# Loading q and v for two pairs of heads at once, copying the unit matrix on chip, halving the last output block, and writing the whole order out

## The chip, the cores and the metric

The kernel runs on one core of a Trainium2 chip. Five engines work side by side, each through its own list of instructions in a fixed order: TensorE (PE; PEld are its weight loads), VectorE (DVE), ScalarE (ACT), GpSimd (POOL) and SyncE (SP), which here does nothing but issue DMAs. The metric is the device time of one execution in microseconds. Three runs of the kernel before took 343.11, 344.51 and 344.69 us, median 344.51.

## The reference

The inputs are q, k and v of 4 batches with 8 heads of 576 rows and 64 columns, a routing matrix `moe_phi`, two expert weights and two weights of a dense layer. Three steps follow each other:

```
attn = softmax(mask(q @ k.T / 8)) @ v        # window of 32; heads 4 to 7: every 4th position of 128
x    = attn laid out as (2304, 512)
logits = x @ phi                             # 32 slots, 8 experts of 4
slots  = softmax(logits, over tokens).T @ x
out_s  = relu(slots @ w1[e]) @ w2[e]         # w1: 8 x 512 x 1024, w2: 8 x 1024 x 512
x    = softmax(logits, over slots) @ out_s   # (2304, 512)
h    = x @ w_in                              # w_in (512, 2048), w_out (2048, 512) in 64 bits
out  = silu(h) @ w_out
```

## The kernel before

**Stages.** The first stage is attention over 16 pairs of heads, n = 0 to 15. For each pair three loads bring k, q and v, 288 KB each (`lk`, `lq`, `lv`: lines 167, 171, 184); POOL and DVE spread q over two halves (`qx`, `qy`, line 180) and v (`vx`, `vy`, lines 197 to 201); PE adds a mask and multiplies (`M`, `S`); DVE takes the row maximum (`rm`, line 227); ACT exponentiates nine blocks (`ex`, line 232); DVE inverts the sums (`rc`, lines 244 and 245), POOL scales (`nm`, line 249), DVE transposes in four pieces (`pt`, lines 256 to 263); PE multiplies by v (`pv`); ACT copies out (`xe`), PE transposes with a unit matrix (`T`, line 312), ACT copies again (`te`). In between the logits of a batch are reduced over tokens (`da` to `ds`) and over slots: `cad` (lines 412 to 414) takes the sum over slots and its inverse, `caf` and `cag` make two parts, `cb` transposes them on PE (line 434) and `cbs` copies them into the tile `ct`. The second stage is the experts: `L1.0` to `L1.15` and `L2.0` to `L2.15` on PE, each with one 1024 KB weight tile (`lw1`, `lw2`, lines 530 and 536; the last tile of w2 in three parts, `lw2.15`, `lw2b`, `lw2c`). The third is the dense layer. Its 64-bit weights come in by `lwi` and `lwo` (lines 620, 625), DVE turns them into 32-bit numbers in three passes (lines 634, 636, 638: `cva`, `cvb`, `cvi` for w_in and `cvc`, `cvd`, `cvo` for w_out), PE multiplies w_in by the expert outputs (`aqh0`, `aq0`, `aqr0`, later `aq1`, `aq3`, ...; rows `w_wif,lg`), ACT and DVE write the result in two parts (`ah`, `al`), and PE forms h in blocks (`h`, `ch`; rows `ct_ct,rv_astk`) and the products with w_out (`on`, `om`, and `pp` for the last 1536 tokens, where sums of weights and activations replace eight products by seven).

**What sets the order.** Each engine runs its instructions in the order in which they are emitted. Up to the middle of the experts that order comes from a list scheduler in the kernel file (costs, a table of bonuses); from `L2.5` on it is written out as a list of names, `LATER`. The loads stand in a list of their own. A load waits for its place in SBUF: the slots of raw q, k and v are reused after two to five pairs, those of the weights after the tile that was there before.

**Unit matrix and end.** One load, `cip` (line 1174), brings a 128x256 tile `ip`: phi, and a 128x128 unit matrix in 32 bits. The same matrix in 16 bits comes with the mask (`cmask`, line 1123). At the end two 128x384 blocks are summed by DVE (`pe1.6.0`, `pe1.6.1`, line 1116) and each is stored by one DMA (line 1119).

Of the kernel before, what the change touches and what calls it, by code (L numbers as in the profile page):

```python
# [32 lines left out]
def fused_kernel(ctx: ExitStack, tc: tile.TileContext, a: dict):  # L33
# [298 lines left out]
    for n in range(NPAIR):  # L332
        b, p = divmod(n, 4)
        kb, rb = before(kslot, n), before(rslot, n)
        qb, vb = before(qslot, n), rb if n < NPAIR - 1 else None
# [1 line left out]
        op(f"lq{n}", "SP", .74, [f"qx{qb}", f"qy{qb}"] if qb is not None else [], lambda n=n: load_q(n))
        op(f"lv{n}", "SP", .74, [f"vx{vb}", f"vy{vb}"] if vb is not None else [], lambda n=n: load_v(n))
        for z in range(2):
            op(f"q{'xy'[z]}{n}", "DVE" if z and n not in QP else "POOL", .7, [f"lq{n}", f"S{n-2}" if n >= 2 else None], lambda n=n, z=z: spread(n, z))  # L340
        for z in range(2):
            op(f"v{'xy'[z]}{n}", veng(n) if z else "POOL", {"POOL": 1.4, "ACT": .68, "DVE": .745}[veng(n) if z else "POOL"], [f"lv{n}", f"pv{n-2}.1" if n >= 2 else "izm", ("nm0", "rc0")[z] if n == 1 else None], lambda n=n, z=z: vmask(n, z))
# [838 lines left out]
    op("crs", "POOL", .9, ["cip", "nm3"], crs)  # L1181


    wl_ = [f"lw1.{i}" for i in range(16)] + [f"lw2.{i}" for i in range(16)] + ["lw2b", "lw2c"]
    il = [f"lwi0.{k}" for k in range(2)]
    ol = ["lwo0", "lwo1"]
    loads = ["lq0", "lk0", "cmask", "lq1", "lk1", "cip", "lv0", "lq2", "lk2", "lv1"]
    vs = [f"lv{n}" for n in range(2, NPAIR)]
    n = 3
    for c in ATT:  # L1190
        if c == "q":
            loads += [f"lq{n}", f"lk{n}"]
            n += 1
        else:
            loads.append({"w": wl_, "v": vs, "i": il, "o": ol}[c].pop(0))
    assert n == NPAIR and not vs + wl_ + il + ol
    loads += ["lwi1.0", "lwo2", "lwi2.0", "lwo4", "lwi3.0", "lwo6", "lwi4.0", "lwo8", "lwi5.0", "lwo10", "lwi6.0", "lwo12", "lwi7.0", "lwo14"]
    assert len(loads) == len(set(loads)) == sum(o[0] == "SP" for n, o in ops.items()) - 6 - 16
    for x, y in zip(loads, loads[1:]):
        ops[y][2].append(x)  # L1200
# [69 lines left out]
LATER = """  # L1270
L2.5 cb2.1 cbs2.1 L2.6 ht1 lwo1 cb2.0 hr1 L2.7 lwi0.0 cvc0 L2.8 L2.9 cvd0 caf3 lw2.14 cvc1 L2.10 cva0.0 lw2.15 lw2b L2.11 ani L2.12 cvo0
cbs2.0 wh0 cvb0.0 L2.13 cvd1 wl0 L2.14 lw2c cvo1 L2a lwi0.1 cvi0.0 lwi1.0 L2b wh1 lwo2 wl1 L2.15 cag3 ts0.1 soe0 cb3.1 soe1 ts0.2 lwi2.0
ts0.4 th0.2 cva0.1 sotm0 sote0 sotm1 aqh0 tl0.2 sote1 cvb0.1 aq0 cvi0.1 ah0 al0 aqr0 h0.0.0 gh0.0.0 h0.0.1 cva1.0 ahr0 gh0.0.1 si0.0.0
cvb1.0 alr0 si0.0.1 cvi1.0 cvc2 on0.0.0 gl0.0.0 on0.2.0 lwo4 cb3.0 on0.1.0 h0.1.0 aq1 gh0.0.2 cbs3.1 lwi3.0 cbs3.0 si0.0.2 gl0.0.1 h0.1.1
om0.0.0 ah1 cvd2 gl0.0.2 ac2.0 gh0.1.0 cvo2 om0.1.0 on0.5.0 om0.2.0 on0.3.0 om0.3.0 si0.1.0 gl0.1.0 ac2.1 wh2 cva2.0 on0.4.0 om0.4.0 lwo6
am1 om0.5.0 al1 om0.0.1 ac2.2 ac3.0 ac2.3 ac3.3 wl2 om0.1.1 om0.2.1 h0.2.0 cva3.0 ac3.1 h0.2.1 om0.3.1 om0.4.1 gh0.2.0 om0.5.1 cvb2.0
on0.1.2 cvb3.0 si0.2.0 gl0.2.0 on0.0.2 ac3.2 on0.3.2 h0.3.0 h0.3.1 om0.0.2 on0.5.2 on0.2.2 si0.3.0 om0.1.2 gh0.3.0 om0.2.2 cvi3.0 cvi2.0
cvc4 om0.3.2 gl0.3.0 aq3 ah3 on0.4.2 om0.4.2 am3 om0.5.2 om0.0.3 om0.1.3 ac4.1 cvd4 al3 cvo4 lwi4.0 cva4.0 lwo8 cvc6 ac4.2 om0.2.3 ac5.1
ac4.0 ac5.3 ac4.3 wh4 h0.4.0 h0.4.1 gh0.4.0 ac5.0 om0.3.3 ac5.2 om0.4.3 wl4 om0.5.3 si0.4.0 cvd6 on0.5.4 on0.1.4 ac7.0 ac6.2 h0.5.0 gl0.4.0
h0.5.1 lwi5.0 gh0.5.0 cvo6 on0.0.4 si0.5.0 gl0.5.0 ac6.3 ac6.0 wh6 on0.3.4 om0.0.4 on0.4.4 om0.1.4 on0.2.4 om0.2.4 om0.3.4 cvb4.0 ac6.1  # L1280
om0.4.4 om0.5.4 wl6 ac7.3 om0.0.5 h0.6.0 h0.6.1 gh0.6.0 si0.6.0 cvi4.0 om0.1.5 om0.2.5 ac7.2 gl0.6.0 cva5.0 om0.3.5 om0.4.5 cvb5.0 lwo10
ac7.1 om0.5.5 h0.7.0 h0.7.1 om0.0.6 om0.1.6 om0.2.6 gh0.7.0 si0.7.0 om0.3.6 cvi5.0 aq5 cvc8 gl0.7.0 cvd8 ah5 cvc10 om0.4.6 cvo8 am5 al5
lwi6.0 ac8.0 ac8.2 ac8.3 ac9.0 om0.5.6 ac8.1 om0.0.7 om0.1.7 wh8 ac9.1 lwo12 om0.2.7 h0.8.0 h0.8.1 om0.3.7 si0.8.0 om0.4.7 om0.5.7 gh0.8.0
ts2.1 cvd10 ac10.3 ac9.3 ac9.2 wl8 cvo10 on0.2.8 on0.0.8 gl0.8.0 ac11.3 ac10.2 h0.9.0 h0.9.1 on0.1.8 gh0.9.0 ts1.1 on0.5.8 on0.4.8 om0.0.8
# [237 lines left out]
```

## Time and profile before

| what | us |
|---|---|
| three runs | 343.11, 344.51, 344.69 |
| the profiled execution, its own time | 343.64 |
| its span in the trace | 341.5 |
| PE busy in the span | 329.4 (96%) |
| DVE busy | 263.3 (77%) |
| ACT busy | 221.9 (65%) |
| POOL busy | 74.6 (22%) |

Around the span lie 2.1 us (343.64 less 341.5). The profiled execution is 0.9 us under the median of the three runs, and between the fastest and the slowest of them. Ends of matmuls are modelled in the trace, so a busy PE can hide a short wait; the start times of the next rows tell it.

### The profile page before, as it was taken

Reading aid. Unit: us, or ns where it says so; the run is one execution under the profiler, and the core shown is the slowest. Engines: PE = TensorE matmul, PEld = TensorE weight load, DVE = VectorE, ACT = ScalarE, POOL = GpSimd, SP = SyncE. Lnnn points to the kernel's source line nnn. Section 1 sums busy time; section 2 is a strip of 40 time slices with the busy share of each in tenths; the row PEclk is TensorE's granted clock in tenths of the full one; section 3 lists DMA queues with packets and bytes.
Section 4 is the critical chain, followed back from the end, with each engine's and each line's share of the span. In section 5 each row is a group of like instructions: output and inputs, shape, how many; then the busy total and the mean of one; then the engine's idle time right before and its main releaser. Section 6 shows DMA issues by size and latency. Waiting matters only on the chain.

```text
span 341.5 us, 8179 instructions
## 1 busy us (share of the span) xinstructions
PE 329.4 (96%) x3221; PEld 272.1 (80%) x3232; DVE 263.3 (77%) x479; ACT 221.9 (65%) x639; POOL 74.6 (22%) x121
## 2 busy tenths in 40 slices
PE   7998999999899999999999999999999999999995
PEld 3687877777633337788888888999999999999995
DVE  5777877689660099999999997989994654999573
ACT  3599989797430125778496999996467666645540
POOL 6987978675260000000000000000000000000000
PEclk9999999999999999999999999999999999999999
DMA  7999999999999999818390000110200011000004
GB/s 259 405 405 406 403 401 407 416 404 415 416 405 423 416 411 419 349 58 322 125 356 15 0 0 2 55 68 2 77 3 0 0 71 69 3 23 23 2 22 147
DMA packets 17893, 70.03 MB, mean 205 GB/s; under 512 B 1984, under 2 KB 4288, under 8 KB 12096
## 3 DMA queue, kind: packets, MB, share of 16 engines
q1 hardware_dynamic: 17856, 69.53, 51.9%
q8 instruction: 25, 0.41, 0.5%
q14 instruction: 12, 0.10, 0.1%
HBM read 64.80 MB, written 4.72 MB: 204 GB/s over the span
## 4 chain that ended last, share of the span: by engine, by line
PE 83%; DMA 8%; DVE 3%; ACT 2%; POOL 1%; issue 1%; DVEq 0%; ACTq 0%; POOLq 0%
PE ps L86 80%; DMA w_w2.13_1760<-in_w 5%; PE ps L312 3%; DMA w_wi<-in_w_in 3%; ACT rt_px L232 1%; DMA rs_raw<-in_q 1%; POOL rv_v L1138 1%; ACT rt_px L301 1%; POOL rb_a L180 0%; PE ps L434 0%; POOL ra_a L180 0%; ACT x_xb L315 0%; DVE stats L227 0%; DVE csm L413 0%; DVE spaced L244 0%
## 5 line engine op out<-in xcount | busy, mean ns | idle before, releaser
L1083 DVE TENSOR_TENSOR rt_stl<-w_raww,rs_sth 128x768 fp32r<-128x768 f32 (+1 forms) x52 | 42.2, 830 | 18.2 <-ACT rs_sth L1081 17.9
L86 PE MATMUL ps<-w_ws,x_gz 128*128 128x512 f32 x216 | 53.6, 393 | 0.0
L86 PE MATMUL ps<-rs_sth,w_ws 128*128 128x384 f32 x192 | 53.1, 334 | 0.0
L1081 ACT CAST rs_sth<-w_raww 128x768 fp32r<-128x768 f32 (+1 forms) x52 | 37.8, 738 | 22.3 <-PE ps L86 16.6
L232 ACT ACTIVATE rt_px<-ps,spaced 128x64 f32<-128x64 f32 x144 | 43.5, 332 | 10.2 <-DVE spaced L228 8.5
L86 PEld LDWEIGHTS ps<-w_ws,x_gz 128*128 128x128 f32 x216 | 40.0, 188 | 7.7 <-issue 0.4
L86 PEld LDWEIGHTS ps<-rs_sth,w_ws 128*128 128x128 f32 x192 | 35.1, 188 | 0.0
L232 ACT ACTIVATION_READ_ACCUMULATOR rt_px<-ps,spaced 128x1 f32 x144 | 32.3, 225 | 0.0
L86 PE MATMUL ps<-rt_stl,w_ws 128*128 128x384 f32 x96 | 32.1, 334 | 0.0
L86 PE MATMUL ps<-ct_ct,rv_astk 128*128 128x384 f32 x96 | 27.3, 338 | 0.0
L1066 ACT ACTIVATE w_raww<-ps 128x384 f32<-128x384 f32 x48 | 22.0, 493 | 7.1 <-PE ps L86 7.0
L249 POOL TENSOR_TENSOR rt_px<-rt_px,stats 128x576 f32<-128x576 f32 (+2 forms) x17 | 18.6, 1093 | 8.2 <-DVE stats L245 3.4
L86 PEld LDWEIGHTS ps<-ct_ct,rv_astk 128*128 128x128 f32 x96 | 17.6, 188 | 2.4 <-issue 0.4
L86 PEld LDWEIGHTS ps<-rt_stl,w_ws 128*128 128x128 f32 x96 | 18.0, 188 | 0.0
L896 ACT ACTIVATE x_gz<-ps 128x768 fp32r<-128x768 f32 (+3 forms) x18 | 13.3, 740 | 4.8 <-PE ps L86 4.7
L899 DVE TENSOR_TENSOR x_gz<-rt_gtm,x_gz 128x768 fp32r<-128x768 f32 (+3 forms) x18 | 15.5, 864 | 1.0 <-ACT rt_gtm L889 0.9
L1081 ACT CAST rs_sth<-x_rawx 128x768 fp32r<-128x768 f32 x12 | 10.0, 837 | 9.6 <-PE ps L86 6.3
L889 ACT ACTIVATE rt_gtm<-ps 128x768 f32<-128x768 f32 (+3 forms) x18 | 13.2, 742 | 3.8 <-PE ps L86 3.6
L86 PEld LDWEIGHTS ps<-ra_a,rv_v 128*64 128x64 f32 x320 | 13.3, 137 | 2.8 <-issue 1.1
L86 PE MATMUL ps<-ra_a,rv_v 128*64 128x96 f32 (+2 forms) x320 | 14.9, 241 | 0.4 <-DVE ra_a L263 0.3
L1083 DVE TENSOR_TENSOR rt_stl<-x_rawx,rs_sth 128x768 fp32r<-128x768 f32 x12 | 11.5, 954 | 4.7 <-ACT rs_sth L1081 4.6
L315 ACT COPY x_xb<-ps 128x640 f32<-128x640 f32 x16 | 11.3, 708 | 5.7 <-PE ps L312 3.5
(298 smaller groups left out, 772.2 us busy)
## 6 DMA issues: line engine op xcount, KB each, us to landing
w_wi<-in_w_in SPq DMA_DIRECT2D x7, 1024.0 KB, 7.1
rs_wo<-in_w_out SPq DMA_DIRECT2D x4, 1024.0 KB, 5.8
rk_k<-in_k SPq DMA_DIRECT2D x12, 288.0 KB, 7.6
w_wo<-in_w_out SPq DMA_DIRECT2D x3, 1024.0 KB, 4.7
rs_raw<-in_v SPq DMA_DIRECT2D x9, 288.0 KB, 9.4
rs_raw<-in_q SPq DMA_DIRECT2D x8, 288.0 KB, 6.5
w_more<-in_q SPq DMA_DIRECT2D x8, 288.0 KB, 9.4
w_more<-in_v SPq DMA_DIRECT2D x6, 288.0 KB, 8.0
```

The costliest lines, as they stand in the source:

```text
L86: pe.matmul(out, lhsT=lhsT, rhs=rhs, start=start, stop=stop, skip_group_check=True)
L232: act.activation(out=preg(n)[:, j, :], in_=sj(n, j), func=ACTF.Exp, scale=D ** -0.5, bias=nmx[:, r, j // 3, j % 3:j % 3 + 1], accum_out=su ...
L249: pool.tensor_tensor(out=p, in0=p, in1=rinv[:, n % 2, j0:j1].rearrange("p (j o) -> p j o", o=1).to_broadcast([128, j1 - j0, 64]), op=ALU.mult)
L301: act.copy(out=x, in_=src)
L312: pe.transpose(ps[0:m, c:c + 128], x[:, 128 * t:128 * t + m], ident)
L315: act.copy(out=xreg(n)[:, :, 0:128], in_=ps[:, TC:TC + 640].rearrange("p (t c) -> p t c", c=128))
L889: act.activation(out=cols(gt(f), x), in_=hbs(x), func=ACTF.Silu)
L896: act.activation(out=cols(gbuf(f, 0), x), in_=hbs(x), func=ACTF.Silu)
L899: dve.tensor_tensor(out=gsl(gbuf(f, 1), x), in0=gsl(gt(f), x), in1=gsl(gbuf(f, 0), x), op=ALU.subtract)
L1066: op(f"cs{x}", "ACT", .385, [f"ch{x}", *d], lambda c=c, b=b, i=i, s=s: act.activation(out=at(c, b, i), in_=bank[6 + s][:, 0:TW], func=ACTF ...
L1081: op(f"sh{x}", "ACT", cost(c, PRODS[p][0], j, .42, .74), [*src, old, "cvo14" if o < 0 else None], lambda c=c, p=p, j=j: both(c, p, j, 0, l ...
L1083: lambda c=c, p=p, j=j: both(c, p, j, 1, lambda x, h, l: dve.tensor_tensor(out=l, in0=x, in1=h, op=ALU.subtract)))
```

## The change

Four things change.

- From the fifth pair on (n = 4), q of two pairs is one DMA of 128 rows of 1152 numbers, and so is v up to pair 13. k stays one DMA for each pair. The inputs are laid out on the host to fit. Six q loads and five v loads of 576 KB take the place of 22 loads of 288 KB. Such a load waits until both slots are free.
- `cip` brings phi alone (64 KB). The 32-bit unit matrix is copied on DVE from the 16-bit one (`idn`).
- The last output block, `pe1.6.1`, is summed and stored in two halves of 192 columns (the second is `pe1.10.1`).
- The scheduler is gone: one list, `ORDER`, names every operation from the first to the last, the DMAs included.

```
+    def lead(n, last):
+        return n if n < 4 or n >= last else n - n % 2
+
+    def load_two(raw, src, n, last):
+        x, y = src[n // 2], raw(n)
+        if lead(n + 1, last) != n:
+            sp.dma_start(out=y, in_=x[:, S * (n % 2):S * (n % 2) + S])
+        else:
+            sp.dma_start(out=raw(n, 2), in_=x)
+
     def load_q(n):
-        b, p = divmod(n, 4)
-        sp.dma_start(out=qraw(n), in_=a["q"][b, p])
+        load_two(qraw, a["q"], n, NPAIR)
...
     def load_v(n):
-        b, p = divmod(n, 4)
-        sp.dma_start(out=vraw(n), in_=a["v"][b, p])
+        load_two(vraw, a["v"], n, VLAST)
...
-    op("cip", "SP", .37, [], lambda: sp.dma_start(out=ip, in_=a["ip"]))
+    op("cip", "SP", .21, [], lambda: sp.dma_start(out=ip[:, 0:128], in_=a["phi"]))
+    op("idn", "DVE", .2, ["cmask"], lambda: dve.tensor_copy(ident, identb))
...
+                    cuts = ((0, TW // 2), (TW // 2, TW)) if last_ and m else ((0, TW),)
+                    for h, (n0, n1) in enumerate(cuts):
...
-        first = [n for n in list_schedule(ops) if n not in set(later)]
-        assert len(first) + len(later) == len(ops)
-        for name in first + later:
+        order, done = ORDER.split(), set()
+        for name in order:
             ops[name][3]()
+            done.add(name)
...
-LATER = """
-L2.5 cb2.1 cbs2.1 L2.6 ht1 lwo1 cb2.0 hr1 L2.7 lwi0.0 cvc0 L2.8 L2.9 cvd0 caf3 lw2.14 cvc1 L2.10 cva0.0 lw2.15 lw2b L2.11 ani L2.12 cvo0
+ORDER = """
+iza1 iza0 ifl iq1 iq0 pex fl0 izb0 iq4 it0 iq2 iq3 lq0 lq1 qx0 lk0 qy0 cmask izb1 S0 M0 lq2 lk1 lv0 rm0 izm ex0.8 ex0.0 ex0.1 qx1 vy0 ex0.2
```

Two places show how instructions move. The line numbers of the changed file are 1 to 17 higher than those of the file before.

The first is DVE near the end of attention, between the row maximum of the last pair and the transposes of the last but one. Before: `csm` and the first `cmx` are `cad0` and `caa1`, `ra_a` are the four transposes `pt14`, `stats` the inverse sums of pair 15 (`rc15.0`).

```order
L412 TENSOR_REDUCE csm<-cn 128x5
L413 TENSOR_SCALAR csm<-csm 128x5
L414 RECIPROCAL csm<-csm 128x5
L472 TENSOR_REDUCE cmx<-lg 128x5
L381 TENSOR_REDUCE hsb<-ps 1x32
L256 STREAM_TRANSPOSE ra_a_108<-rt_px 64x9x32
L397 TENSOR_TENSOR le<-lg,ps 128x160
L258 STREAM_TRANSPOSE ra_a_108<-rt_px 64x9x32
L244 TENSOR_SCALAR spaced<-stats 128x2x3
L245 RECIPROCAL stats<-spaced 128x6
L260 STREAM_TRANSPOSE ra_a_108<-rt_px 64x9x32
```

The same place on DVE now; `rv_v` is `vy14`, the half of v of pair 14 that DVE makes.

```order
L239 TENSOR_SCALAR spaced<-stats 128x3x3
L267 STREAM_TRANSPOSE ra_a_108<-rt_px 64x9x32
L269 STREAM_TRANSPOSE ra_a_108<-rt_px 64x9x32
L271 STREAM_TRANSPOSE ra_a_108<-rt_px 64x9x32
L274 STREAM_TRANSPOSE ra_a_108<-rt_px 64x8x32
L212 TENSOR_SCALAR rv_v<-rs_raw,zm 128x9x64
L255 TENSOR_SCALAR spaced<-stats 128x2x3
L256 RECIPROCAL stats<-spaced 128x6
L426 TENSOR_REDUCE csm<-cn 128x5
L427 TENSOR_SCALAR csm<-csm 128x5
L428 RECIPROCAL csm<-csm 128x5
```

The four transposes of pair 14 now follow each other, and `cad0` stands behind them, between the two inversions of pair 15; `vy14` moved from before them to behind them.

The second place is PE at the end of the experts and the start of the dense layer. Before: `w_w2.15` is the last tile of w2, `ip,cc` the transposes `cb3.1` (two rows) and `cb3.0` (three), `s_62,x_sip` the step `sotm`, `w_wif,lg` the products `aqh0`, `aq0` and `aqr0`, `ct_ct` the first blocks of h, `rk_ws,x_gz` the first products with w_out.

```order
L86 MATMUL ps<-w_w2.15_1828,x_sip 32x256 x4
L86 MATMUL ps<-w_w2.15_1828,x_sip 32x128 x8
L434 MATMUL ps<-ip,cc 128x128
L434 MATMUL ps<-ip,cc 128x64
L86 MATMUL ps<-s_62,x_sip 128x32 x4
L86 MATMUL ps<-w_wif_1826,lg 32x128 x32
L86 MATMUL ps<-ct_ct,rv_astk 128x384 x2
L86 MATMUL ps<-rk_ws_1843,x_gz 128x512 x4
L434 MATMUL ps<-ip,cc 128x128 x3
L86 MATMUL ps<-rk_ws_1843,x_gz 128x512 x2
```

The same place on PE now.

```order
L87 MATMUL ps<-w_w2.15_1807,x_sip 32x256 x4
L448 MATMUL ps<-ip,cc 128x128 x3
L87 MATMUL ps<-w_w2.15_1807,x_sip 32x128 x8
L87 MATMUL ps<-s_62,x_sip 128x32 x4
L87 MATMUL ps<-w_wif_1826,lg 32x128 x16
L448 MATMUL ps<-ip,cc 128x128 x3
L87 MATMUL ps<-w_wif_1826,lg 32x128 x16
L87 MATMUL ps<-ct_ct,rv_astk 128x384
L448 MATMUL ps<-ip,cc 128x128
L448 MATMUL ps<-ip,cc 128x64
L87 MATMUL ps<-ct_ct,rv_astk 128x384
L87 MATMUL ps<-rk_ws_1815,x_gz 128x512 x2
```

The transposes of `cc` moved: `cb2.0` between the parts of the last w2 tile, `cb3.0` between the two halves of the `w_wif` products, `cb3.1` between the first two blocks of h; and after the first product with w_out (two matmuls, `on0.0.0`) PE now goes to the next block of h (`h0.1.0`) where it went on with more products.

## Rows read from the trace of the kernel before

**Rows 1.** The page, sections 1 and 2: busy time; 40 slices of clock and DMA.
```profile
PE 329.4 (96%) x3221; PEld 272.1 (80%) x3232; DVE 263.3 (77%) x479; ACT 221.9 (65%) x639; POOL 74.6 (22%) x121
...
PEclk9999999999999999999999999999999999999999
DMA  7999999999999999818390000110200011000004
```

**Rows 2.** The chain of waits that ended last: start us, us, what.
```profile
79.14 0.33 DVE csm L412
79.50 0.76 DVE csm L413
...
80.28 0.19 DVE csm L414
...
118.52 10.18 DMA w_wi<-in_w_in
...
128.72 0.43 DVE w_wif L634
...
134.21 203.75 PE ps L86 x1167
...
337.99 0.56 DVE lg L1116
```

**Rows 3.** Stretches: us, busy of each engine (instructions), PE clock, DMA share, GB/s.
```profile
20.00:60.00 40.00, 38.07 (x805) 31.22 (x805) 30.40 (x80) 36.64 (x179) 33.10 (x48) 1.00 1.03 403
...
97.00:126.00 29.00, 29.00 (x265) 9.96 (x261) 9.60 (x23) 6.43 (x14) 4.07 (x6) 1.00 1.01 413
126.00:132.00 6.00, 5.49 (x107) 3.66 (x100) 5.62 (x12) 2.07 (x7) 0.00 (x0) 1.00 1.01 418
...
141.50:180.00 38.50, 38.50 (x228) 31.48 (x227) 37.52 (x40) 28.32 (x60) 0.00 (x0) 1.00 0.63 232
```

**Rows 4.** Timeline, 118 to 142: start, us, engine, line, instruction, idle before and its releaser.
```profile
127.48 0.16 PEld L86 LDWEIGHTS ps<-w_w2.15_1828,x_sip 128*32 128x32 f32 x8 [0.37 <-DMA w_w2.15_1828<-in_w]
...
129.41 1.08 PE L86 MATMUL ps<-w_wif,lg 128*32 128x128 f32 x32
...
130.12 0.69 DVE L638 SCALAR_TENSOR_TENSOR w_wif<-w_wi,w_wif 128x512 uint32<-128x512 uint32 x1
...
130.87 1.08 PE L86 MATMUL ps<-w_wif,lg 128*32 128x128 f32 x32 [0.38 <-DVE w_wif L638]
...
131.88 0.62 PE L86 MATMUL ps<-ct_ct,rv_astk 128*128 128x384 f32 x2
...
132.69 1.19 PE L86 MATMUL ps<-rk_ws,x_gz 128*128 128x512 f32 x4 [0.19 <-ACT x_gz L896]
...
133.72 0.49 PE L434 MATMUL ps<-ip,cc 128*128 128x128 f32 x3
...
133.96 0.71 PE L86 MATMUL ps<-rk_ws,x_gz 128*128 128x512 f32 x2
```

**Rows 5.** DMA issues: transfer, queue, count, KB each, median us to landing.
```profile
rs_raw<-in_q SPq DMA_DIRECT2D x8, 288.0 KB, 6.5
w_more<-in_q SPq DMA_DIRECT2D x8, 288.0 KB, 9.4
...
ip<-in_ip SPq DMA_DIRECT2D x1, 128.0 KB, 5.0
```

**Rows 6.** Timeline of PE, 96 to 98: the first expert tile.
```profile
96.66 1.06 PE L86 MATMUL ps<-ct_w1.0_283,x_sip 128*32 128x512 f32 x8
```

**Rows 7.** Timeline of DVE, 77 to 97: transposes of the last two pairs.
```profile
80.78 0.46 DVE L256 STREAM_TRANSPOSE ra_a<-rt_px 64x288 f32<-64x288 f32 x1
...
83.84 0.44 DVE L263 STREAM_TRANSPOSE ra_a<-rt_px 64x256 f32<-64x256 f32 x1
...
86.70 0.27 DVE L263 STREAM_TRANSPOSE rb_a<-rt_px 64x96 f32<-64x96 f32 x1
```

**Rows 8.** Timeline of SP, 336 to 342: issues of the last stores.
```profile
338.57 0.33 SPq L1119 DMA_DIRECT2D out<-lg  x1
```

More of the change, by code (lines that the diff above doesn't have):

```diff
@@ L28 @@
 JH = 6
+VLAST = NPAIR - 2
 CBANK = ((2, 1), (5, 1), (4, 6), (5, 1))
@@ L334, in fused_kernel @@
         kb, rb = before(kslot, n), before(rslot, n)
[L335 removed]
+        qn, vn = lead(n, NPAIR), lead(n, VLAST)
+        two = lambda x, slot: [f"{x}{c}{m}" for c in "xy" for m in [before(slot, n)] + ([before(slot, n + 1)] if lead(n + 1, VLAST if x == "v" else NPAIR) == n else []) if m is not None and (x == "q" or n < NPAIR - 1)]
         op(f"lk{n}", "SP", .74, [f"S{kb}"] if kb is not None else [], lambda n=n: load_k(n))
[L337 to L338 removed]
+        if qn == n:
+            op(f"lq{n}", "SP", (.74, 1.43)[lead(n + 1, NPAIR) == n], two("q", qslot), lambda n=n: load_q(n))
+        if vn == n:
+            op(f"lv{n}", "SP", (.74, 1.43)[lead(n + 1, VLAST) == n], two("v", rslot), lambda n=n: load_v(n))
         for z in range(2):
[L340 removed]
+            op(f"q{'xy'[z]}{n}", "DVE" if z and n not in QP else "POOL", .7, [f"lq{qn}", f"S{n-2}" if n >= 2 else None], lambda n=n, z=z: spread(n, z))
         for z in range(2):
[L342 removed]
+            op(f"v{'xy'[z]}{n}", veng(n) if z else "POOL", {"POOL": 1.4, "ACT": .68, "DVE": .745}[veng(n) if z else "POOL"], [f"lv{vn}", f"pv{n-2}.1" if n >= 2 else "izm", ("nm0", "rc0")[z] if n == 1 else None], lambda n=n, z=z: vmask(n, z))
         free = [exn(n - 2) if n >= 2 else None, ex1(n - 1) if n else None]
@@ L622, in load_wo @@
     def load_wo(f, n):
-        t = tiles[f"wo{f//2}"] if f % 2 else new(WOS[f // 2 % 2], f"wo{f//2}")
+        t = tiles[f"wo{f//2}"] if f"wo{f//2}" in tiles else new(WOS[f // 2 % 2], f"wo{f//2}")
         o = 1024 * (f % 2)
@@ L824, in fused_kernel @@
                 op(f"ac{f}.{r}", "ACT", .31, [f"ah{q}" if r < 2 else f"al{q}"], lambda f=f, r=r: ac(f, r))
-    op("ani", "ACT", .25, ["L2.6", "cip"], ani)
+    op("ani", "ACT", .25, ["L2.6", "idn"], ani)
     for f in range(16):
@@ L1179, in crs @@
             pool.tensor_copy(s4[32 * g:32 * g + 32], eye)
[L1181 to L1200, printed above, removed]
+    op("crs", "POOL", .9, ["idn", "nm3"], crs)
     CHB = {n: k % 2 for k, n in enumerate(hist)}
@@ L1258, in emit_all @@
     def emit_all():
-        later = LATER.split()
-        first = [n for n in list_schedule(ops) if n not in set(later)]
-        assert len(first) + len(later) == len(ops)
-        for name in first + later:
+        order, done = ORDER.split(), set()
+        assert sorted(order) == sorted(ops)
+        for name in order:
+            assert done.issuperset(ops[name][2]), name
             ops[name][3]()
+            done.add(name)
     with tc.manual_schedule():
         emit_all()
-LATER = """
@@ L1275 @@
[L1275 to L1278, printed above, removed]
@@ new lines @@
+ex14.1 ex14.2 ex14.3 ex14.4 dt2 pv12.1 ex14.5 dm2 pt13.3 ds1 ex14.6 M15 qx15 ex14.7 rc14 caa0 xe12 nm14 S15 db2 lv15 dsub2 T12 rm15 dex2
+vx14 pv13.0 lw1.15 te12 ex15.0 ex15.1 dq2 pt14.0 ex15.2 lt12 ex15.3 pv13.1 pt14.1 pt14.2 pt14.3 ex15.4 xe13 dc2 ex15.5 cab0 ex15.6 cac0
+ex15.7 lw2.0 ex15.8 vy14 T13 rc15.0 cad0 nm15.0 rc15.1 te13 pv14.0 pt15.0 pt15.1 pt15.2 pv14.1 pt15.3 cae0 xe14 nm15.1 lt13 dr2 vy15 caf0
+pt15.4 dw2 T14 vx15 lw2.1 cag0 pt15.5 pv15.0 pt15.6 lw2.2 te14 dwe2 pv15.2 pt15.7 dacc2 pv15.1 cb0.0 caa1 lt14 ds2 cab1 xe15 lw2.3 cac1 caa2
```

262 lines of the change are left out of this document (88 added, 174 removed).

## The prediction

> **What bounds the kernel now.** I read the busy times first, then the chain of waits, then the stretches, then the timeline where the stages meet. The reader is to see three stages with different limits. PE is busy 96% of the span, its clock is at full speed in all 40 slices (the upper level, 2.4 GHz), and the DMA engines are full in the first 17 slices [rows 1]. The chain ends with one piece of PE work of 203.75 us from 134.21 to 337.96; the last DVE addition and the last store follow [rows 2]. In the middle of it, 141.5 to 180, PE is busy for all of 38.5 us [rows 3], and the waits of PE have no row from 141.5 to 338: nothing can be won there by moving instructions, something only lost. So a gain has to come from before 134 or from the last 3.5 us.
>
> Before 134 two lines of work arrive together. One is the DMA stream: 403 GB/s from 20 to 60, 413 from 97 to 126 [rows 3], and its last piece that matters, the second half of the first w_in tile, is issued at 118.52 and there at 128.70; DVE starts to turn it into numbers at 128.72, and PE waits for the end of that, 0.38 us, until 130.87 [rows 2, 4]. The other is PE itself: the experts start at 96.66 [rows 6] and run without a pause, 29.00 of 29.00 us from 97 to 126 [rows 3], up to the last part of the last w2 tile, whose weight load waited 0.37 us for its DMA until 127.48 [rows 4]. PE alone would thus have been there at 127.11. Neither line gains without the other: an earlier stream wins 0.37 us, and more only by as much as attention ends earlier than 96.66.
>
> **The change part by part.**
>
> *Double loads.* 22 loads of 288 KB (6.49 MB) become 11 of 576 KB. Their rows in memory grow from 2304 to 4608 bytes; a weight row has 8192. About half of the bytes from 20 to 60 are weight tiles, half such short rows. If that half goes at 413 GB/s, the short rows go at 393.5 (the two averaged in time per byte give 403 [rows 3]). Taking the time of a row as a fixed part plus a part by bytes, the two rates give a fixed part of 0.385 (ns times bytes per ns of the whole stream), and twice the length saves half of it: 0.385 x (1/2304 - 1/4608) = 0.0000835 ns a byte, or 0.54 us for 6.49 MB. Bounds: nothing, if the difference between the two stretches is not the rows' length; 0.78 us, if the new rows go at 413 altogether. I take 0.54. The row shows a time per byte that is 5% longer for short rows. The Trainium skill ("DMA: Bandwidth & Descriptors", section "Why small descriptors are slow") gives a fixed overhead of about 3 cycles for each packet beside one for each 32 bytes; by that, an estimate from the page, a row of 2304 bytes costs 75 cycles and half a row of 4608 only 73.5, 2% of the 16.1 us that these bytes take at 403, or 0.32 us, and the sum below would be 0.4 instead of 0.6. The trace here speaks for the larger figure. What a double load costs is time of arrival: the first of its pairs comes with the second, and both slots must be free. The loads are issued 6 to 9 us before they land [rows 5], since the stream is backed up; the slots that they wait for (two to four pairs earlier) are free before the stream would come to them, so I cost this at nothing. Without that cover the price is one 288 KB load, 0.73 us at 403 GB/s, at PE's first product of a pair.
>
> *Unit matrix.* 64 KB less in the stream, half of the 128 KB row [rows 5]: 0.16 us at 403 GB/s. The copy on DVE and the clearing of a PSUM part that now stands beside it lie near 16 us, ahead of the transposes of pair 1; no trace shows this copy, and between nothing and 0.5 us of DVE are absorbed there, as v's half moves back by 0.8 us in exchange.
>
> *Order of attention.* DVE spends 1.33 us on `cad0` (79.14 to 80.47) and then starts `pt14` at 80.78, whose four pieces are pulled apart by three other steps and end at 84.28 [rows 2, 7]. Now they follow each other: four pieces of about 0.46 take 1.9 us where 3.5 passed. But `vy14` (0.8 us, the length of such a step elsewhere) comes behind them, and PE's product of pair 14 needs it; so about 0.8 us of the 1.6 are left there. `cad0` then delays the second half of pair 15. I put the end of attention 0.5 us earlier, with bounds of 1.5 earlier and 2.1 later; late next is pair 15 on DVE, whose last transpose ended at 86.97 [rows 7].
>
> *Front, together.* Stream: 0.54 + 0.16 = 0.70. PE: 0.37 + 0.5 = 0.87. The smaller counts: 0.70 earlier at the `w_wif` products. Bounds: 0 and 0.94 (0.78 + 0.16), and a loss where attention is late (below).
>
> *Start of the dense layer.* `cb3.0` costs PE 0.24 us at 133.72 to 133.96, in the dense part [rows 4]; it moves to where PE waits for DVE (0.38 us), so 0.24 is won. `cb3.1` moves into the gap before the first product with w_out. Against that: the next block of h now stands right behind the first product. ACT has to read two more parts of h for it, in four to five steps, where before PE had 0.9 us of other products to do. I count an idle 0.7 us there, of which 0.4 is made up since the block and its ACT work come earlier. Together a loss of 0.05; bounds 0.6 gained (both gaps closed) and 0.7 lost.
>
> *Last block.* The DVE step takes 0.56 us from 337.99 [rows 2], its store is issued at 338.57 [rows 8]. A half takes between 0.28 and 0.56; the first store goes out about 0.2 us earlier. The second has to wait for SP, which took 0.33 us for the issue [rows 8] and needs some more between two: it goes out near 338.8, 0.2 later than the whole now, and moves half of 192 KB, 0.24 us less at 403 GB/s. Sum 0, bounds 0.25 gained and 0.3 lost.
>
> *The dense part from 141.5.* Nothing to win. In it DVE is busy 37.52 of 38.5 us [rows 3], so the same steps in another order can make PE wait; I take 0, bounds 0 and 0.8 lost.
>
> Sum: -0.70 + 0.05 + 0 = -0.65 us, against the profiled execution 343.64 - 0.65 = 343.0. That execution is 0.87 us under the median of the runs; on the median's side it is 344.51 - 0.65 = 343.9 us.
>
> **The rivals.**
>
> A, the forecast: 343.9.
>
> B, more is won. The stream goes at the weights' rate (-0.94), attention ends at least 0.6 us earlier, both gaps at the start of the dense layer close (-0.6), the last store wins 0.25: -1.8, or 342.7. For it: the gaps of 0.38 and of 0.51 us (132.18 to 132.69) are there, and the new order puts transposes in both [rows 4]. Against it: the next block of h directly behind the first product.
>
> C, the change doesn't do what it says: rows of 4608 bytes move no faster, and only the 64 KB go: -0.16, or 344.4. For it: short loads stand in the stretch with 403 GB/s together with a fuller POOL and ACT, so their length need not be the cause. Against it: 413 GB/s wherever weights alone move [rows 3].
>
> D, slower: the end of attention. `cad0` (1.33 us [rows 2]) now stands between the two inversions of pair 15, so the second scaling on POOL, the last transposes on DVE and PE's last product come later by 1.3 to 2.1 us (`cad0`, and `vy14` with it). It decides once the experts start more than 0.37 us after 96.66; beyond that the whole kernel moves, since PE has no pause afterwards. The loss is 1.3 - 0.37 = 0.93 to 2.1 - 0.37 = 1.73, in the middle 1.35: 345.9. For it: DVE is on the chain of waits there. Against it: pair 14 is done earlier in the same order.
>
> **How the numbers follow.** A 0.42, B 0.24, C 0.15, D 0.19. A measurement of this kernel can tell about 0.5%, 1.72 us, from no change: under 342.8 is faster, over 346.2 slower. B lies at the lower bound and gives 0.17 to faster, A 0.07 by its bounds; D gives 0.09 to slower, the bounds of A and C 0.02. So 0.24 faster, 0.65 no change, 0.11 slower. The range takes in B and D with the spread of their bounds, and the runs' own spread of 1.6 us: 342.0 to 345.9.
>
> **What would show it.** In the changed profile: the half tile of w_in landing near 128.0 and the second `w_wif` group starting near 130.2; 405 to 408 GB/s from 20 to 60; the first expert tile before 96.4; the long PE piece with no waits after 141; the last store's issue near 338.2 (0.65 earlier, 0.2 later). D shows as a start of the experts after 97.0, C as an unchanged landing at 128.7. The forecast is wrong if PE waits appear between 141 and 338, or if the stream runs dry somewhere before 130.

## The result, and the profile of the changed kernel

The changed kernel takes 346.92 us in the median of 6 runs (345.73 to 348.59), the kernel before 343.81 in 6 runs beside it (343.11 to 344.69). The ratio is 1.0089, with an interval from 1.0065 to 1.0113: 3.1 us slower, where 0.65 us faster was forecast. The profiled execution is the longest of the six, 348.59 us with a span of 346.8, so distances in its trace are larger than those of the medians: its span is 5.3 us above that of before.

The page of the changed kernel, sections 1 and 2 [rows 1]:

```profile
span 346.8 us, 8162 instructions
...
PE 334.6 (96%) x3222; PEld 274.6 (79%) x3232; DVE 261.6 (75%) x481; ACT 220.9 (64%) x639; POOL 74.7 (22%) x121
...
PEclk9999999999969999999999999999999999999999
DMA  7999999999979999954654000110100030001004
```

PE is busy 5.2 us longer with all but the same products. The row of the clock says where: in the twelfth slice, 95 to 104 us, there is a 6. The same place in stretches of 1 us (the columns are those of [rows 3]):

```profile
93.00:94.00 1.00, 0.37 (x3) 0.26 (x2) 0.70 (x4) 0.24 (x1) 0.45 (x2) 1.00 1.08 418
94.00:95.00 1.00, 0.00 (x0) 0.13 (x2) 0.41 (x1) 0.10 (x1) 0.70 (x1) 0.82 0.99 401
95.00:96.00 1.00, 0.83 (x3) 0.27 (x2) 0.00 (x0) 0.00 (x0) 0.00 (x0) 0.50 0.98 410
...
100.00:101.00 1.00, 1.00 (x5) 0.61 (x5) 0.52 (x2) 0.00 (x0) 1.00 (x3) 0.50 0.96 401
101.00:102.00 1.00, 1.00 (x8) 0.60 (x11) 0.67 (x3) 0.34 (x1) 1.00 (x1) 0.77 0.47 197
```

PE does nothing from 93.37 to 95.17, and within that pause the granted clock drops to 0.50, the lower level (1.2 GHz); by the means of 0.82 and 0.77 in the stretches at either end it is there from 94.6 to 101.5. What PE waited for is in the timeline of the end of attention:

```profile
92.97 0.40 PE L87 MATMUL ps<-hsb,ones 1*128 1x32 f32 x2
...
93.92 0.49 DVE L432 TENSOR_TENSOR cc<-cn,chi 128x320 f32<-128x320 f32 x1
94.01 0.70 POOL L436 COPY cc<-chi 128x320 f32<-128x320 f32 x1 [0.56 <-DVE chi L431]
94.77 0.13 PEld L87 LDWEIGHTS <-cc 128*128 128x128 bf16 x2 [1.51 <-POOL cc L436]
95.17 0.64 PE L87 MATMUL ps<-cc 128*128 128x512 bf16 x1 [1.80 <-POOL cc L436]
...
97.22 2.53 PE L87 MATMUL ps<-x_xb,le 128*32 128x129 f32 x40
...
101.65 1.06 PE L87 MATMUL ps<-ct_w1.0_257,x_sip 128*32 128x512 f32 x8
```

The waiting product is a filler. `fill` multiplies the tile `cc`, read as bf16, with itself into a PSUM part that nobody reads; it is there to keep PE busy. `cc` is also what the steps `caf1` (DVE, L432) and `cag1` (POOL, L436) write. In the order written out, `ff0` and `ff1`, the first two groups of fillers, now stand behind `cag1`. In the kernel before they stood ahead of both writers, as its timeline shows:

```profile
92.21 0.38 PE L86 MATMUL ps<-cc 128*128 128x512 bf16 x1 [0.16 <-issue]
...
93.08 0.60 PE L86 MATMUL ps<-cc 128*128 128x512 bf16 x2
...
93.70 1.45 PE L86 MATMUL ps<-x_xb,le 128*32 128x129 f32 x40
93.80 0.49 DVE L418 TENSOR_TENSOR cc<-cn,chi 128x320 f32<-128x320 f32 x1
93.82 0.78 POOL L422 COPY cc<-chi 128x320 f32<-128x320 f32 x1 [1.11 <-DVE chi L417]
```

So in the changed kernel a product whose result is worth nothing waits for POOL, and everything on PE waits behind it. The same 40 products with `x_xb` that took 1.45 us in the kernel before take 2.53. The experts start at 101.65 instead of 96.66 [rows 6], 4.99 later, and the kernel never gets that back. By steps: the last transposes of pair 15 come 0.52 later than before, the product behind the wait 2.97, the first expert tile 4.99; that is 0.5 of attention, some 2.45 of waiting with its start-up, and 2.0 at the lower clock.

The other stretches [rows 3]:

```profile
0.00:20.00 20.00, 17.29 (x219) 10.73 (x222) 11.43 (x33) 9.08 (x49) 15.17 (x35) 1.00 0.93 350
20.00:60.00 40.00, 37.52 (x782) 30.45 (x782) 29.72 (x78) 35.45 (x175) 28.86 (x40) 1.00 1.02 407
60.00:80.00 20.00, 19.60 (x414) 16.26 (x416) 16.44 (x48) 17.53 (x84) 16.09 (x26) 1.00 1.00 380
...
97.00:126.00 29.00, 29.00 (x266) 11.25 (x269) 7.85 (x21) 5.31 (x12) 4.75 (x6) 0.92 0.89 354
...
141.50:180.00 38.50, 38.50 (x228) 31.02 (x227) 37.76 (x40) 29.30 (x64) 0.00 (x0) 1.00 0.60 223
```

Between 20 and 60 the stream moves 407 GB/s, where 405 to 408 was the sign for the double loads; but 380 follows. The chain ends as before with one piece of PE work, 204.60 us instead of 203.75 [rows 2]:

```profile
138.60 204.60 PE ps L87 x1169
```

### The profile page after: what moved, and what is told of

The parts are those of the page before. It is cut to its first block, busy times and chain, and to the rows that moved or that the text cites. A ratio compares the mean times of both kernels' runs of the same rounds, so it can differ in the third digit from the quotient of the medians.

```text
span 346.8 us, 8162 instructions
## 1 busy us (share of the span) xinstructions
PE 334.6 (96%) x3222; PEld 274.6 (79%) x3232; DVE 261.6 (75%) x481; ACT 220.9 (64%) x639; POOL 74.7 (22%) x121
## 4 chain that ended last, share of the span: by engine, by line
PE 90%; ACT 3%; DVE 2%; issue 1%; POOL 1%; DMA 1%; SPq 0%; DVEq 0%; POOLq 0%; ACTq 0%
PE ps L87 86%; PE ps L323 3%; ACT rt_px L243 2%; DMA rk_k<-in_k 1%; PE ps L448 1%; POOL rt_px L260 1%; ACT x_xb L326 0%; DVE cc L432 0%; SPq L178 0%; DVE stats L238 0%; POOL cc L436 0%; POOL ra_a L192 0%; ACT rt_px L310 0%; POOL rv_v L208 0%; ACT x_gz L910 0%
## 5 line engine op out<-in xcount | busy, mean ns | idle before, releaser
L1080 ACT ACTIVATE w_raww<-ps 128x384 f32<-128x384 f32 x48 | 22.7, 493 | 10.2 <-PE ps L87 9.4
L87 PE MATMUL ps<-ct_ct,rv_astk 128*128 128x384 f32 x96 | 28.4, 341 | 0.2 <-ACT rt_gtm L903 0.2
L238 DVE TENSOR_REDUCE stats<-ps 128x9 f32<-128x576 f32 x16 | 11.8, 739 | 6.7 <-PE ps L87 5.5
L87 PEld LDWEIGHTS ps<-rb_a,rv_v 128*64 128x64 f32 x320 | 13.0, 137 | 3.4 <-issue 1.3
L87 PE MATMUL ps<-rb_a,rv_v 128*64 128x96 f32 (+2 forms) x320 | 14.4, 242 | 1.2 <-ACT rt_px L243 0.7
```

The lines of the kernel that those rows point to most:

```text
L87: pe.matmul(out, lhsT=lhsT, rhs=rhs, start=start, stop=stop, skip_group_check=True)
L238: dve.tensor_reduce(out=mxs[:, n % 2], in_=ps[:, c:c + 64 * NJ].rearrange("p (j c) -> p j c", c=64), axis=AXX, op=ALU.max)
L1080: op(f"cs{x}", "ACT", .385, [f"ch{x}", *d], lambda c=c, b=b, i=i, s=s: act.activation(out=at(c, b, i), in_=bank[6 + s][:, 0:TW], func=ACTF ...
```

## The experiments

Theory W: the loss is the filler's wait for `cag1` and the half clock that follows it. Theory F: it comes from the front, the first loads in another order and a late stream. All ratios are to the kernel before, run on the same chip in turns, and take in all runs of both; the times are medians.

**e1, the filler reads another tile.**

```diff
-            mm(bank[b], fsrc[:, 0:128], fsrc[:, 0:512], True, True)
+            mm(bank[b], src[:, 0:128], src[:, 0:512], True, True)
...
```

(`src` is the mask tile for `ff0` to `ff2`)

> The changed kernel, with one thing different: the short filler products that keep PE busy at the end of attention read the mask tile, which nothing writes after the first microseconds, in place of the tile cc, which the step cag1 on POOL writes just before. Theory W (the loss sits in the filler: 1.80 us of waiting for POOL, and the half clock from 94.8 to 101.2 that follows it): the wait is gone, the clock stays at full, the experts start near 97.2 (0.5 later than before, as the last transposes of pair 15 are), the time falls to 343.5 to 344.8 us, a ratio to the kernel before of 1.000 to 1.004. Theory F (the loss comes from the front: the first loads in another order and a stream that is 0.7 late): the experts still start after 98.5 and the ratio stays at 1.006 or more.

343.62 us, ratio 1.0014 (0.9992 to 1.0035): W. Against the changed kernel's 1.0089 that is 0.75%, 2.6 us. The runs spread from 342.76 to 346.69, and the profiled one is the longest: no wait for POOL is left at the end of attention, the clock is at 1.00 there, but attention itself ends late and the experts start at 99.81, not at 97.2. A start after 98.5 was F's sign, so in this execution F holds as well. Seven of the twelve runs lie at 342.8 to 343.8 and five at 344.7 to 346.7, all with a granted clock of 0.998 or more: something besides the filler lengthens some executions and not others. Whether it is the front, e4 takes up.

**e2, the wait stays, PE is kept busy in it.**

```diff
-        op(f"ff{k}", ... lambda b=b, c=c: fill(c, b))
+        op(f"ff{k}", ... lambda k=k, b=b, c=c: (fill(0 if k else 8, b, maskid), fill(c, b)))
```

> The changed kernel, with 8 more filler products that read the mask tile ahead of the first one that reads cc: PE has 1.7 us of work while the wait for POOL lasts, but everything behind still starts only when cag1 is done. It parts the wait from the clock. Theory W: the granted clock stays at full, the experts start near 99.2 to 99.6 (the 2.4 us of the wait and its overhead and the 0.5 of attention remain, the 2.1 to 2.3 us of half clock go), ratio 1.003 to 1.007. If the clock falls for another reason than the pause of 1.8 us, it falls here too: experts at 101.5, ratio 1.008 to 1.010.

345.91 us, ratio 1.0069 (1.0048 to 1.0090). In its trace the fillers on the mask tile (the profile calls it `hsb` here) reach up to the wait's end (start, us, engine):

```profile
92.78 1.67 PE L87 MATMUL ps<-hsb 128*128 128x512 bf16 x7 [0.16 <-issue]
94.29 0.59 PE L87 MATMUL ps<-cc 128*128 128x512 bf16 x2
...
98.44 1.07 PE L87 MATMUL ps<-ct_w1.0_257,x_sip 128*32 128x512 f32 x8
```

and by the stretch from 93 to 97 the granted clock is 1.00:

```profile
93.00:97.00 4.00, 4.00 (x53) 2.06 (x51) 1.28 (x6) 0.63 (x2) 0.71 (x1) 1.00 1.00 412
```

From the last product ahead of the wait (92.22) to the experts it takes 6.2 us, in the changed kernel (92.97 to 101.65) 8.7: the half clock was 2.5 us there. Over all runs it is 0.20% or 0.7 us, with an uncertainty of 1.1, and what is left over e1, the wait, 0.55% or 1.9 us. The clock is not lost every time: of the changed kernel's six runs one has a mean clock of 1.000 and still takes 346.25 us, the other five have 0.988 to 0.993 and take 345.73 to 348.59. So an execution can be that slow without the lower clock; what the clock adds in the mean is not settled closer than that, nor which of the two is the larger part.

**e3, the kernel before with the filler late.**

```diff
+        late = ["ff0", "dr3", "ff1", "dw3", "dwe3", "dc3"]
+        first = [n for n in first if n not in late]
+        i = first.index("cag1") + 1
+        first[i:i] = late
```

> The kernel before, with its first two filler products and the products behind them written after the step cag1, as in the changed kernel; nothing else is moved. Theory W: PE waits 1.5 to 2.2 us for POOL near 93, the clock falls to half behind it, the experts start 3.5 to 5 us late (100.2 to 101.7), ratio 1.007 to 1.013, although loads, unit matrix and last block are those of before. Theory F: the experts start at most 1 us late, ratio under 1.003.

346.01 us, ratio 1.0069 (1.0057 to 1.0081): the loss moves, at the low end of W, into the kernel before with loads, unit matrix and last block untouched. (`dacc3` comes ahead of `dwe3` here, so the last batch is scaled by an older weight; the work is the same.) The timeline of its wait:

```profile
93.41 0.11 PEld L86 LDWEIGHTS <-cc 128*128 128x128 bf16 x2 [1.51 <-POOL cc L422]
93.64 0.58 PE L86 MATMUL ps<-cc 128*128 128x512 bf16 x1 [1.63 <-DVE mrun L394]
...
99.34 1.06 PE L86 MATMUL ps<-ct_w1.0_283,x_sip 128*32 128x512 f32 x8
```

The stretch behind the wait, at 0.50:

```profile
94.00:97.00 3.00, 3.00 (x33) 1.89 (x36) 0.31 (x2) 0.29 (x1) 0.00 (x0) 0.50 1.00 418
```

The releaser of the second row is an inference; the row of the weight load names POOL. The experts start 2.7 us late, a little less than expected.

**e4, e1 with the first loads of the kernel before.**

```diff
-iq2 iq3 lq0 lq1 qx0 lk0 qy0 cmask izb1 S0 M0 lq2 lk1 lv0
+iq2 iq3 lq0 lk0 cmask lq1 qx0 qy0 izb1 S0 M0 lq2 lk1 lv0
```

> As e1, and the first loads on SP in the order of the kernel before (q of pair 0, k of pair 0, mask, q of pair 1). Theory W with the front as a second, smaller term: the first scores start 0.9 earlier than in the changed kernel, the second 1.5 earlier; the end of attention comes 0 to 1 us earlier than in e1 (experts at 96.2 to 97.2), ratio 0.997 to 1.003. If the start is absorbed by the middle of attention, no difference to e1 over 0.2 us at the start of the experts.

343.15 us, ratio 0.9991 (0.9982 to 1.0000), with runs from 342.67 to 344.07: e1's long executions are gone. The changed kernel's first scores wait for k, which is now the third load (timeline of PE):

```profile
5.66 2.19 PE L87 MATMUL ps<-rk_k,ra_a 128*64 128x64 f32 x36 [0.88 <-DMA rk_k<-in_k]
```

Before the first scores start at 4.70, in e4 at 4.71. The second start at 10.40 in the changed kernel, at 8.90 before and 8.76 in e4. The experts of e4 start at 96.12, 0.54 ahead of before; the tiles of w2 land 0.81 to 0.83 ahead from 85 to 115. (Some 0.16 of that, by estimate, are the 64 KB less of `cip`.) Then more than half of the lead is lost, on SP (its timeline):

```profile
101.54 0.33 SPq L550 DMA_DIRECT2D w_w2.12_1723<-in_w  x1
110.41 0.80 SPq L639 DMA_DIRECT2D w_wo<-in_w_out  x2
```

and the stretch behind it moves 299 GB/s:

```profile
112.00:114.00 2.00, 2.00 (x24) 0.54 (x19) 0.00 (x0) 0.69 (x1) 0.00 (x0) 1.00 0.90 299
```

The w2 tile 13, which the kernel before issued at 102.94, now stands behind the loads of w_out, and these wait for a product. The stream runs dry at 112, and the second half of the first w_in tile lands at 128.40, only 0.30 ahead of before.

**e5 to e8.** e6 puts the w2 tile 13 back; e5 is e6 with single loads; e7 is the kernel before with q of pair 1 ahead of k of pair 0; e8 is e6 with `caf0` behind pair 15's transposes.

```diff
e6: -... lw2.12 L1.14 ... L2.6 lw2.13 cvd0    +... lw2.12 lw2.13 L1.14 ... L2.6 cvd0
e5: -return n if n < 4 or n >= last else n - n % 2    +return n        (and lq4 -> lq4 lq5, and so on)
e7: +first.remove("lq1"); first.insert(first.index("lk0"), "lq1")
e8: -vy15 caf0 pt15.4 dw2 T14 vx15 lw2.1 cag0    +vy15 pt15.4 ... pt15.7 caf0 cag0 ... T15 cb0.0
```

> As e6, but q and v of each pair in a load of its own, both loads where the double one stood: only the rows' length is undone (2304 instead of 4608 bytes). Theory D (a row of 4608 bytes costs some 8 ns less than two of 2304, as the packets of the changed kernel's trace show, 178 against 2 x 93): over 1408 such rows on 16 engines the stream is 0.70 us later from 70 on than in e6, the second half of the first w_in tile lands 0.5 to 0.8 later, the time is 0.2 to 0.7 us longer than that of e6. Theory N (the rows' length changes nothing, the stream's gain came from the order): landings within 0.2 us of those of e6, time the same.

> As e4, and the load of the w2 tile 13 again ahead of the two loads of w_out and the first of w_in, which wait on SP for the expert's product L1.14, as in the kernel before. In e4 the stream is 0.7 us ahead of before until 111, then falls to 299 GB/s at 112 to 114 and is only 0.3 ahead at the first w_in tile. Theory S (SP's queue is the reason): no fall under 390 GB/s from 100 to 126, that tile's second half lands 0.6 to 0.8 us ahead of the kernel before (near 127.6), PE reaches the second group of w_wif 0.4 to 0.6 ahead, ratio to before 0.997 to 0.999. Rival: the stream is stopped by the buffers, not by SP's order; then the landing stays at 127.9 and the ratio is that of e4 (0.999).

> The kernel before, with one load moved: q of pair 1 ahead of k of pair 0, as in the changed kernel. Theory W's second term (front): the first scores start 0.5 to 0.9 later, the second 0.8 to 1.5 later, and since attention of before has less slack the experts start 0.5 to 1.5 late, ratio 1.002 to 1.005. Rival: the middle of attention absorbs it, ratio under 1.001.

> As e6, and the DVE step caf0 (1.08 us with its sub-steps) behind the last transposes of pair 15 instead of between them, with POOL's cag0 and PE's cb0.0 behind it. Theory P (DVE's transposes of pair 15 are what ends attention): they end 0.8 to 1.1 us earlier, the experts start 0.5 to 1.0 us earlier than in e6; the time is 0 to 0.5 us shorter, since the stream then decides the start of the dense layer. Rival: cag0 and cb0.0 are late for caf1, PE waits near the end of attention, and the experts start no earlier.

e6: 344.42 us, ratio 1.0027 (1.0018 to 1.0037), slower than e4. Theory S was half right: the stream no longer falls (415 GB/s from 97 to 126), and that half tile lands at 126.82 instead of 128.70. But PE now waits for something that I had not counted (its timeline):

```profile
130.84 0.86 PE L87 MATMUL ps<-w_wif,lg 128*32 128x128 f32 x24 [1.35 <-DVE w_wif L652]
```

DVE turns w_out and w_in into numbers in one row of steps that needs w_out first. The w2 tile ahead of w_out starts that row at 119.25 instead of 117.84 in e4, and its steps come 1.4 later up to the first half of w_in (127.09 against 125.69). This execution is e6's fastest (343.59 us, its experts start at 94.83), and its second group of `w_wif` products still starts no earlier than that of before (130.84 against 130.87, 130.59 in e4); in the traces of e8 and e5, closer to their medians, it starts at 131.90 and 132.05. Behind the stream and PE, DVE is a third line that arrives at the same place.

e8: 344.51 us, ratio 1.0027 (1.0016 to 1.0038), the same as e6, with the same 1.35 us of wait for `w_wif`, as if what attention wins could not pass DVE. That it won something there, as theory P had it, is not shown: its experts start at 95.76, those of e6's fastest execution at 94.83. Differences of under 1 us at this place can't be read from one trace of each version. e5: 345.22, ratio 1.0050 (1.0036 to 1.0065), 0.8 us over e6, slightly more than theory D's 0.2 to 0.7, and not N. e7: 343.54, ratio 1.0008 (0.9994 to 1.0023). In its trace the first scores start 1.30 late, the second 0.60, the experts 0.11: the rival, the middle of attention absorbs it in this kernel, though its runs reach from 343.01 to 345.59 where those of before end at 344.62.

**e9, both lines together.**

```diff
 e4, caf0 cag0 cb0.0 as in e8, and:
-hr0 caa3 lw2.12 L1.14 ... ht1 hr1 lwi0.0 caf2
+hr0 caa3 lw2.12 lwi0.0 L1.14 ... ht1 hr1 caf2
```

> As e4 (the w2 tile 13 where the changed kernel has it), with two moves: caf0, cag0 and cb0.0 behind pair 15 as in e8, and the first w_in load on SP ahead of the two w_out loads, since it waits for an earlier product (L1.11 instead of L1.14). Theory T (three lines meet at the first w_in products: PE, the stream, and DVE's conversions, which need w_out early): the experts start 0.8 to 1.0 ahead of the kernel before, no fall of the stream at 112, DVE's conversions start within 0.6 of e4's 117.8, the second group of w_wif starts near 130.2 (0.6 ahead of before, 0.3 ahead of e4), ratio 0.996 to 0.999. Rival: the w_out loads, now behind w_in, hold DVE's conversions up as the w2 tile did in e6 (PE waits over 1 us for w_wif), ratio 1.001 or more.

343.25 us, ratio 0.9989 (0.9980 to 0.9997): no different from e4. The experts start 0.78 ahead of before, but w_out lands behind w_in, DVE's row starts at 119.11, and PE waits 0.54 for `w_wif`. The rival's mechanism, at half its price.

**e10, no filler.**

```diff
-TAIL = (("dt3", 2, 0), ("dr3", 2, 3), ("cb1.1", 1, 3))
+TAIL = ()
...
```

(and the fillers' names are gone from `ORDER` and from what `dr3` waits for)

> As e4, without the three groups of filler products at the end of attention (PE does 1.2 us less). Theory K (the fillers hold the clock; a pause of PE of under 1 us here is enough to lose it): the granted clock falls to half for some us between 92 and 100, the experts start 1 to 2.5 us later than in e4, ratio 1.002 to 1.008. Rival: the products around them hold the clock by themselves; the experts start 0 to 0.6 us earlier than in e4, ratio 0.997 to 0.999, and the loss in the changed kernel was bought for nothing.

342.98 us, ratio 0.9999 (0.9977 to 1.0020), runs from 342.29 to 346.53. In the profiled one (344.71) the experts start at 95.71, 0.4 ahead of e4, and lose it: the granted clock is 0.50 from 94.65 to 98.07 (the stretch from 95 to 97 is shown) and the first tile's 8 products take 1.94 us instead of 1.07.

```profile
95.00:97.00 2.00, 2.00 (x12) 0.77 (x14) 1.42 (x3) 0.34 (x1) 2.00 (x3) 0.50 1.00 418
```

Neither theory as it stood: three of the twelve runs have a mean clock of 0.995 (343.83, 344.71 and 346.53 us), the other nine 0.998 or more (342.29 to 345.21). Without fillers the clock can be lost, and was in this execution, but the median is not longer.

**e11, the repair by order alone.** The fillers read `cc` as they did.

```diff
-dt3 cae1 lw2.4 dm3 la3 cb0.1 db3 te15 lw2.5 dsub3 caf1 dq3 dex3 cag1 ff0 dr3 ff1 dw3
+dt3 ff0 cae1 lw2.4 dm3 la3 cb0.1 db3 te15 lw2.5 dsub3 dq3 dr3 ff1 caf1 dex3 cag1 dw3
```

(and the first loads as in e4)

> The changed kernel with its fillers still reading cc, repaired by order alone: the first filler right behind the product it follows, the second ahead of caf1, which writes cc, as in the kernel before; first loads as in e4. Theory W: what made the fillers wait was that they stood behind the writer of the tile they read; PE waits for nothing from POOL at the end of attention, the clock stays at full, the experts start within 0.3 of e4's 96.1, ratio 0.998 to 1.001. If reading cc were itself the cost, whatever the order, the ratio stays over 1.004.

342.98 us, ratio 0.9980 (0.9971 to 0.9989), runs from 342.43 to 343.33: the fastest steady version, 0.64 us under the kernel before in the medians and by the ratios 3.7 under the changed one. The experts start at 96.05, 0.61 ahead of before. Its timeline of PE has no idle time there:

```profile
91.23 0.60 PE L87 MATMUL ps<-cc 128*128 128x512 bf16 x2
...
92.61 0.61 PE L87 MATMUL ps<-cc 128*128 128x512 bf16 x2
93.27 1.45 PE L87 MATMUL ps<-x_xb,le 128*32 128x129 f32 x40
...
96.05 1.07 PE L87 MATMUL ps<-ct_w1.0_257,x_sip 128*32 128x512 f32 x8
```

**e12, e11 with single loads** (the edit of e5).

> As e11 (0.998 of the kernel before), with q and v of each pair in a load of its own: the rows' length alone, where neither the filler nor the w2 tile stands in the way. Theory D (8 ns for each pair of rows, 0.70 us of stream): the stream stands 0 to 0.2 us ahead of the kernel before at 90 to 100 (e4 stood 0.65 ahead), the second half of the first w_in tile lands 0.4 to 0.7 later than in e11, the time is 0.2 to 0.7 us longer than e11's, ratio to before 0.999 to 1.001. Theory N: the rows' length changes nothing, landings and ratio are those of e11 (0.998).

343.57 us, ratio 1.0003 (0.9993 to 1.0012): 0.23% over e11, 0.8 us with an uncertainty of 0.5: D, a little over its 0.2 to 0.7. The stretch from 20 to 60, first of e11, then of e12:

```profile
20.00:60.00 40.00, 38.69 (x795) 31.21 (x796) 29.96 (x81) 34.99 (x169) 29.80 (x42) 1.00 1.02 411
```

```profile
20.00:60.00 40.00, 37.58 (x780) 30.58 (x784) 29.44 (x81) 34.46 (x168) 28.85 (x40) 1.00 1.03 406
```

In the traces the w2 tile 2 lands 0.63 later than in e11, the w_in half tile 0.26 later (both streams pause at 112), PE reaches the dense layer 0.27 later. The times say more than the traces because part of the difference lies outside the span. Time less span is 1.82 us in the median of e11's runs and 2.03 in e12's; all versions with double loads have 1.76 to 1.82, e5 with single loads 2.02, the kernel before 2.14 to 2.17. The spans alone differ by 0.5 us in the mean, inside D's range. What happens in those 0.2 us outside no trace shows; single loads are also eleven more DMAs on SP, and no run parts their number from the rows' length.

Against the kernel before, e12 has everything of the change but the double loads, and its ratio is 1.0003: the rest of the change together is worth nothing that can be measured.

## Why the prediction was wrong

**The step that failed** is the term "Order of attention": the end of attention 0.5 us earlier, with bounds of 1.5 earlier and 2.1 later, which stands in the sum as "PE: 0.37 + 0.5". It follows the moved steps of DVE alone. That the fillers `ff0` and `ff1` wait for the writer of `cc`, which the new order puts ahead of them, is a wait that the sum put at nothing without a reason; the prediction does not name the fillers at all. The runs showed in its place, in the profiled execution, the experts 4.99 us late: 0.5 of attention, 2.45 of the wait and 2.0 at the lower clock. The fillers moved behind `cag1` make the kernel before slower by 0.69% (e3); read from another tile or put back ahead of the writer, they leave 1.0014 (e1) and 0.9980 (e11) of the changed kernel's 1.0089. Rival D had the right place (attention's end, experts after 97.03, no pause afterwards to make it good), but less than half of the loss, 1.35 against 3.1, and the wrong mechanism: `cad0` stands where D has it in e11 too, and there the experts start 0.61 early. The range ended at 345.9, the middle of D; nothing in it allowed for this wait or for a lower clock of PE.

**Double loads, 0.54 forecast.** Right in kind and near in size. In the packets of the changed kernel's trace a row of 2304 bytes takes 93 ns in the median and one of 4608 takes 180, 6 ns less than two; 1408 such rows on 16 engines give 0.53 us (in e11 181 ns and 0.44 us). (The 178 ns and 0.70 us in the expectations are from the packets between 62 and 68 us alone.) With single loads the w2 tiles land 0.58 to 0.63 later (e12 against e11) and the spans are 0.5 longer. The Trainium skill's fixed overhead of about 3 cycles a packet ("DMA: Bandwidth & Descriptors", section "Why small descriptors are slow") made it 0.32 by estimate; the measurement here is larger.

**The cover of the double loads** did not hold everywhere. "The stream is backed up" is true while attention is on time. The changed kernel's front is 1.5 us late, so the k slot of pair 11 comes free late: SP issues nothing from 55.22 to 59.93, and the next loads reach a stream that is nearly empty. SP pauses there in other versions of the new order too, and the later the pause ends, the less is moved from 60 to 80: 58.59 and 407 GB/s in e4, 58.63 and 410 in e11, 59.17 and 399 in e2, 59.93 and 380 in the changed kernel, 61.81 and 366 in e1.

**The front** was costed through the unit matrix alone. The move of q of pair 1 ahead of k of pair 0 stood in the same rows and was not costed; it delays the first scores by 0.96 (5.66 against 4.70) and is what parts e1 from e4, 0.23% or 0.8 us, not clear of the measurement (e7: 0.08%). One thing comes on top in some executions. The 36 products of the first scores take 2.19 us in the changed kernel's trace, and 1.27 in that of before:

```profile
4.70 1.27 PE L86 MATMUL ps<-rk_k,ra_a 128*64 128x64 f32 x36
```

In e2, with the same first loads, they start at 5.73 and take 1.27, and the second scores start 0.33 later than before, not 1.50. The trace's first record of the clock comes at 9.31 in the changed kernel, 4.28 before and 4.03 in e2, so the 1.00 in its row for 0 to 20 says nothing of the time ahead of 9.31, and the forecast's "full speed in all 40 slices" nothing of the first 4.28 us of before. The products speak for the lower clock there: the fillers behind the first scores start every 0.43 us up to 8.66 and every 0.21 from 9.42 on. What decides it no run shows.

**The end of attention, 0.5 earlier forecast.** Borne out once the filler is out of the way: 0.54 (e4), 0.61 (e11), 0.38 (e12), in one trace each. The transposes of pair 14 follow each other as forecast (80.88 to 82.76 in the changed kernel), and late next is pair 15 on DVE.

**The stream's dry spell at 112** I had named as a way to be wrong, and it is there in e4; but e6 shows that the place of the w2 tile was worth its price, since DVE's conversions wanted w_out early. That DVE decides there as soon as the stream is early I had not seen: its row of steps is hidden in the trace of before behind the other two lines.

**Dense layer and tail.** No wait of PE from 142 on in the changed kernel either. From the last w2 tile's end to the first full product of w_out, e4 loses 0.17 of its lead, against 0.05 forecast. `cb3.0` does hide between the two groups of `w_wif` products, as forecast (they start 1.48 us apart in e4, 1.46 before), since DVE's last conversion ends at 130.52, just ahead of the second group at 130.59. The loss is at `cb3.1` between the blocks of h: the lead falls from 0.28 at 130.59 to 0.12 at the first product with w_out (132.57 against 132.69). The idle 0.7 us forecast behind that product is 0.16. The rest of the dense part costs 0.16, within the bounds. The last block, in the timeline:

```profile
343.23 0.62 DVE L1133 TENSOR_TENSOR lg<-ps,lg 128x192 f32<-128x192 f32 x2 [0.49 <-PE ps L87]
343.61 0.81 SPq L1137 DMA_DIRECT2D out<-lg  x2
```

From the start of the step to the end of the span it takes 3.57 us in halves, 3.51 before: the first store goes 0.2 earlier, the second's issue ends 0.3 later, and the sum is none, as forecast.

With the filler and the first loads put right (e11) the change is worth 0.64 us in the medians; the forecast sum was 0.65. The signs of A are there (the half tile at 128.08, the second `w_wif` group at 130.26, the experts at 96.05), but that the sums agree so closely is in part luck: the lead of 0.61 at that group is 0.3 at PE's last products, the spans of e11 are 0.2 to 0.4 shorter than those of before (in the median and the mean), and the other 0.35 lies outside the span, where the forecast had no term and no trace can look.

## What to carry to other kernels

A filler that keeps PE busy is an instruction with operands: let it read a tile that nobody writes any more, or keep it ahead of the next writer in the order. When an order is written out anew, compare for each engine not only what stands where but who wrote, last in the new order, each tile that a moved step reads, the tiles of throw-away work too. Where several lines arrive at one point within a microsecond, speeding up one only shows the next; ask of every line what it would wait for.
